# QK-normed attention with a SwiGLU layer behind it: the last four sequences' queries and keys are turned by VectorE and not by TensorE

## The chip, the cores and the metric

The kernel runs on one core of a Trainium2 chip. A core has five engines with a queue of instructions each: TensorE (PE, matmuls into PSUM), VectorE (DVE), ScalarE (ACT), GpSimd (POOL) and SyncE (SP, which here issues DMAs). The queues are in order and wait for each other through semaphores. The metric is the device time of one execution in microseconds; three runs of the kernel before took 1516.35, 1512.67 and 1513.35 us, the median is 1513.35 us. Everything is float32, apart from the weights, which arrive as 64-bit floats.

## The reference, cut to what matters

```python
# attention: 8 sequences, 12 heads, 448 tokens, 64 values to a head
def rmsnorm(x, g):
    rms = np.sqrt(np.mean(x * x, axis=-1, keepdims=True) + 1e-06)
    return x / rms * g
q_n, k_n = rmsnorm(q, g_q), rmsnorm(k, g_k)
scores = matmul(q_n, k_n^T) / sqrt(64)
attn = softmax(scores)                      # over the keys
x = matmul(attn, v)                         # -> 3584 tokens x 768
# SwiGLU layer: 768 -> 1536 -> 768
xn = rmsnorm(x, rms_g)
g = xn @ w_gate
out = (g / (1 + exp(-g)) * (xn @ w_val)) @ w_out
```

For the scores, TensorE contracts over the 64 values of a head. So q and k must lie with these values along the partitions and the tokens along the free axis, while in memory a token's 64 values lie side by side: each head's q and k has to be turned.

## The kernel before, in words

**Steps.** The unit of attention is a pair of heads, g = 0 to 47, six to a sequence (`NPAIR`); two heads of 64 values fill the 128 partitions. The main loop makes one step for each pair. From the second sequence on, step g does, in this order: the scores of pair g (seven parts of 64 keys, `step`, matmuls in L659) interleaved with the value matmuls of pair g-1 (L674); then *items* of the layer behind attention for the sequence before (`fill`), taken from a list that is spread evenly over the steps. Most items are one product of a fast matrix multiplication for gate and value (`product`, L1191: eight PE instructions of 128x224), the others are parts of the output projection (`out_quads`, L1532). Results of items are taken out of PSUM by ScalarE copies (L1206) and VectorE sums (L1209, L1212). Three PSUM banks rotate for items (`ps_f`), four for scores (`ps_s`), and one (`ps_m`) is shared by the value sums and by the turning of q and k.

**How q and k get there, before.** For pair g+3, SP loads q and k with the tokens on partitions (`load_pair`: one DMA for q, two for k; 384 of a head's 448 tokens, three tokens to a partition). The remaining 64 tokens of all heads of a sequence, the *rests*, come in six DMAs once a sequence (L441, L448). For pair g+2, `squares` has ScalarE square q and k (L493), VectorE sum over the 64 values (L496) and GpSimd raise to the power -0.5 (L515) and scale q (`norm_q`, L520); k is scaled by ScalarE in six pieces (`norm_k`, L530). The rests have squares, power and scaling of their own (`norm_rests`). For pair g+1, `turn` transposes on TensorE: three 128x128 blocks of q (L545) and one of the rest (L549), which ScalarE copies out to `qT` with the gains multiplied in (L550) and to `kT` (L551), and later three blocks of k (L545, copied out at L553). The scores become `exp` on ScalarE (L664).

**What sets the order.** The order is written out by hand. `pe(fn)` is one turn of TensorE: it writes fn's instructions into the queues and counts turns. `after(n, fn)` writes fn's instructions into the queues n turns later. No scheduler moves anything afterwards; each engine runs its own queue in the order written. The weights, in the form that the fast multiplication needs, are kept in device memory and stream in through SP (L1070, `w<-kept`, `w<-kept_q`) whenever a buffer comes free. From about 270 us on, each step is such a step.

**DMA semaphores.** DMAs that SP and ScalarE issue take eight semaphores in turn (`DMAHW0` to `DMAHW7`), in the order in which they are written down, whichever queue they are in. A DMA's issue waits until the DMA that had its semaphore before, the eighth before it, has landed.

Of the kernel before, what the change touches and what calls it, by code (L numbers as in the profile page):

```python
# [22 lines left out]
NPAIR = H // 2  # L23
# [312 lines left out]
def safe_scores(  # L336
# [24 lines left out]

    NW = 22
    const, small = pool("c_const", 1), pool("c_small", 4)
    qk_pool, v_pool, qn_pool, qkT_pool = pool("c_qk", 3), pool("c_v", 3), pool("c_qn", 1), pool("c_qkT", 2)
    e_pool, tmp, y_pool, rest_pool = pool("c_e", 11), pool("c_tmp", 1), pool("c_y", 3), pool("c_rest", 2)
# [38 lines left out]

    FULL, LAST = slice(0, NK * 128), slice(NK * 128, S)

    def load_pair(g, parts=(0, 1)):

        if g >= NG:
            return  # L410
        b, hp = divmod(g, NPAIR)
        if 0 in parts:
            qk = st["qk", g] = qk_pool.tile([128, 2, 2 * NK * D], F32, name="qk")
            nc.sync.dma_start(out=qk[:, 0].rearrange("p (h n) -> p h n", h=2),
                              in_=q[b, 2 * hp:2 * hp + 2, FULL].rearrange("h (p t) d -> p h (t d)", t=NK))
        qk = st["qk", g]
        for h in range(2) if 1 in parts else ():
            nc.sync.dma_start(out=qk[:, 1].rearrange("p (t h d) -> p h t d", h=2, d=D)[:, 1 - h],
                              in_=k[b, 2 * hp + h, FULL].rearrange("(p t) d -> p t d", t=NK))

    def load_v(g):
        if g >= NG:
            return
        b, hp = divmod(g, NPAIR)
        vt = st["v", g] = v_pool.tile([128, 2, NK, D], F32, name="vt")
        rows = vt.rearrange("p h t d -> p h (t d)")
        if direct(g):
            nc.sync.dma_start(out=rows, in_=v[b, 2 * hp:2 * hp + 2, FULL].rearrange("h (p t) d -> p h (t d)", t=NK))
            return

        for h in range(2):
            nc.sync.dma_start(out=rows[across(h)], in_=v[b, 2 * hp + h, FULL].rearrange("(f p t) d -> p f (t d)", f=2, t=NK))


    def load_rests(b, i, engine):
        if b >= B:
            return
        if i == 0:
            st["rest", b] = rest_pool.tile([128, NPAIR, 2, D], F32, name="rest")
        for h in range(2):  # L440
            engine.dma_start(out=st["rest", b][own(i), :, 1 - h], in_=(q, k)[i][b, h::2, LAST].rearrange("h i d -> i h d"))  # L441

    def load_v_rests(b):
        if b >= B:
            return
        vr = st["vr", b] = rest_pool.tile([128, NPAIR, D], F32, name="vr")
        for h in range(2):
            nc.sync.dma_start(out=vr[across(h)], in_=v[b, h::2, LAST].rearrange("h i d -> i h d"))  # L448

    def norm_rests(b, lo, hi):  # L450

        if b >= B:
            return
        n = hi - lo
        rest = st["rest", b][:, lo:hi]
        sq = tmp.tile([128, n, 2, D], F32, name="sq", tag="sq", bufs=2)
# [27 lines left out]
    def squares(g, i):  # L484

        if g >= NG:
            return
        n = 2 * NK
        if i == 0:
            st["ms", g] = small.tile([128, 2 * n], F32, name="ms")  # L490
        ms = st["ms", g]
        sq = tmp.tile([128, n * D], F32, name="sq", tag="sq", bufs=2)
        nc.scalar.activation(sq, st["qk", g][:, i], ACT.Square)  # L493

        def reduce():
            nc.vector.tensor_reduce(out=ms[:, i * n:(i + 1) * n], in_=sq.rearrange("p (n d) -> p n d", d=D), axis=AX_X, op=ALU.add)  # L496

        if g <= 1:

            return reduce, lambda: rms_qk(g, slice(i * n, (i + 1) * n))  # L500
        after(1, reduce)
        if i == 1:
            if g == 2:

                due[0:0] = [(now["t"] + 2, lambda: rms_qk(g)), (now["t"] + 2, lambda: norm_q(g))]
                return
            after(2, lambda: rms_qk(g))
            after(2, lambda: norm_q(g))

    def rms_qk(g, cols=slice(0, 4 * NK)):  # L510
        if ("rs", g) not in st:
            st["rs", g] = small.tile([128, 4 * NK], F32, name="rs")
        ms = st["ms", g][:, cols]
        nc.gpsimd.tensor_scalar(ms, ms, D * 1e-6, None, ALU.add)
        nc.gpsimd.tensor_tensor(st["rs", g][:, cols], ms, mhalf[:, cols], ALU.pow)  # L515

    def norm_q(g):
        qn = st["qn", g] = qn_pool.tile([128, 2 * NK * D], F32, name="qn")
        for h in range(2):
            (nc.vector if g <= 2 else nc.gpsimd).tensor_tensor(  # L520
                qn.rearrange("p (t h d) -> p h t d", h=2, d=D)[:, 1 - h], st["qk", g][:, 0].rearrange("p (h t d) -> p h t d", h=2, d=D)[:, h],
                st["rs", g][:, h * NK:(h + 1) * NK].unsqueeze(2).to_broadcast([128, NK, D]), ALU.mult)

    def norm_k(g, half):

        if g >= NG:
            return
        for n in range(NK * half, NK * (half + 1)):
            block = st["qk", g][:, 1, n * D:(n + 1) * D]
            nc.scalar.activation(block, block, ACT.Copy, scale=st["rs", g][:, 2 * NK + n:2 * NK + n + 1])  # L530
# [119 lines left out]
    def keys_of(i):  # L650

        at = i % NK * 128 + i // NK * D if i < 2 * NK else NK * 128
        return slice(at, at + D)

    def scores(g, i):

        ps = ps_s.tile([128, 512], F32, name="sc", tag="s")
        for r in (own(0), own(1)):
            nc.tensor.matmul(ps[r, 0:S], lhsT=st["kT", g][r, keys_of(i)], rhs=st["qT", g][r, :], start=True, stop=True)  # L659
        return ps  # L660

    def exps(g, i, ps):
        e = st["e", g, i] = e_pool.tile([128, S], F32, name="e")
        nc.scalar.activation(e, ps[:, 0:S], ACT.Exp)  # L664

    def weighted(g, i):

# [2 lines left out]
            st["av", g] = ps_m.tile([128, 512], F32, name="av", tag="m")  # L670
        for j in range(2):
            r = across(j)
            vt = st["vr", b][r, hp] if i == PARTS - 1 else st["v", g][r, i // NK, i % NK]
            nc.tensor.matmul(st["av", g][own(j), 0:S], lhsT=vt, rhs=st["e", g, i][r], start=i == 0, stop=i == PARTS - 1,  # L674
                             skip_group_check=True)

# [670 lines left out]
    def store(b, n, i, y):  # L1347
        row0 = at = b * S + i * 128 - 64 * (b % 2)
        while at < row0 + 128:
            seq, col = divmod(at, S)  # L1350
            t, p = divmod(col, 128)
            m = min((128 if t < NK else REST) - p, row0 + 128 - at)
            rows, cols = seq * S, slice(n * HALF, (n + 1) * HALF)
            if t < NK:
# [374 lines left out]
    ones = const.tile([128, D], F32, name="ones")  # L1729
    nc.vector.memset(ones, 1.0)  # L1730

    nc.scalar.activation(tmp.tile([128, D], F32, name="sq", tag="sq", bufs=2), ones, ACT.Square)
    mhalf = const.tile([128, 4 * NK], F32, name="mhalf")
# [32 lines left out]
    def warm(n):  # L1766

        ps = ps_m.tile([128, 512], F32, name="warm", tag="m")
        for _ in range(n):
            nc.tensor.matmul(ps[:, 0:128], lhsT=ident, rhs=ident, start=True, stop=True)  # L1770

    def some_rests(g):
        b, hp = divmod(g, NPAIR)
# [31 lines left out]
    for g in range(NG + 1):  # L1805
# [70 lines left out]
            if g < NG:  # L1876
                later_sums(g, 2)
        st["block"] = now["t"]
        after(2, lambda g=g: load_v(g + 2))
        if hp:  # L1880
            fill()
            norm_k(g + 1, 0)
            squares(g + 2, 0)
            squares(g + 2, 1)
            pe(lambda: turn(g + 1, 0))
            norm_k(g + 1, 1)
            some_rests(g)
            fill()
            pe(lambda: turn(g + 1, 1))
# [5 lines left out]
        pe(lambda: turn(g + 1, 0))  # L1895
# [5 lines left out]
        pe(lambda: turn(g + 1, 1))  # L1901
        fill(len(todo))
        begin(b - 1, 16)
        pe(lambda: norm_x(b - 1))
# [42 lines left out]
```

## Time and profile before

| | |
|---|---|
| median of three runs | 1513.35 us |
| span of the profiled execution | 1514.0 us |
| PE busy | 1478.8 us, 98% |
| VectorE, ScalarE, GpSimd busy | 1037.7, 602.2, 741.3 us |
| DMA engines busy, queue of SP | 69.4% of 16 engines' span |

The page lists each engine's busy time, the chain of work that ended last, and the costliest groups of instructions; queries of the trace give the same for a window, a source line or a tile, and a timeline. A row of a group gives the count, the summed busy time and the mean duration of one instruction. Matmuls overlap in the pipeline, so their durations add up to more than the time they take; start times in the timeline tell what a piece of TensorE work takes. In a timeline, `x8` is a run of eight instructions shown as one row.

### The profile page before, as it was taken

The numbers are of one execution on the slowest core, as the hardware profiler recorded it, in microseconds if no ns is written. First come the engines' busy times: TensorE is split into PE (matmuls) and PEld (weight loads), VectorE is DVE, ScalarE is ACT, GpSimd is POOL, SyncE is SP. The second block draws the span as 40 slices with busy tenths as digits, with TensorE's granted clock in tenths as the row PEclk, the third lists the DMA queues.
The fourth block names the chain that finished last, engine by engine and source line by source line (L and its number), as shares of the span: only waits on it lengthen the run. The fifth ranks groups of instructions, "written<-read, shape, count | busy, mean of one in ns | idle before, by whom it ended". The sixth has DMA issues, their size and how long they took to land.

```text
span 1514.0 us, 25709 instructions
## 1 busy us (share of the span) xinstructions
PE 1478.8 (98%) x8732; PEld 1154.0 (76%) x8732; DVE 1037.7 (69%) x1826; ACT 602.2 (40%) x1377; POOL 741.3 (49%) x708
## 2 busy tenths in 40 slices
PE   8999999999899999999999999999999999999997
PEld 4344445678755888878888888768888789899997
DVE  5788999699944697874568555535668655684664
ACT  6856764344323433234343443443542433101100
POOL 6867997556423454564535643445645731021002
PEclk9999999999999999999999999999999999999999
DMA  7758675776667899996558855585558655587675
GB/s 200 227 159 252 174 247 174 228 249 206 224 219 224 266 316 312 301 291 180 163 150 257 244 176 153 165 255 159 153 153 255 216 162 139 165 292 234 174 228 180
DMA packets 302176, 322.51 MB, mean 213 GB/s; under 512 B 81620, under 2 KB 243668, under 8 KB 302036
## 3 DMA queue, kind: packets, MB, share of 16 engines
q1 hardware_dynamic: 301108, 320.58, 69.4%
q8 instruction: 72, 1.18, 0.3%
q14 instruction: 68, 0.56, 0.1%
q10 hardware_dynamic: 800, 0.20, 0.1%
q0 software_dynamic: 128, 0.00, 0.0%
HBM read 266.90 MB, written 53.77 MB: 212 GB/s over the span
## 4 chain that ended last, share of the span: by engine, by line
PE 84%; DVE 8%; DMA 3%; issue 1%; SPq 1%; POOL 1%; ACT 0%; DVEq 0%; POOLq 0%
PE ff L1191 37%; PE ff L1532 13%; PE sc L659 7%; PE av L674 7%; PE ff L1604 6%; PE ff L1461 5%; PE tr L545 2%; PE den L692 1%; PE den L607 1%; PE sc L563 1%; PE av L590 1%; PE ff L1334 1%; DVE l L1406 1%; DMA w<-kept 1%; DVE w L1091 1%
## 5 line engine op out<-in xcount | busy, mean ns | idle before, releaser
L1191 PE MATMUL ff<-x,w 128*128 128x224 f32 x1296 | 259.6, 353 | 1.4 <-DVE pb L1212 1.1
L714 POOL TENSOR_TENSOR es<-es,e 128x448 f32<-128x448 f32 x205 | 253.4, 1236 | 13.6
L1191 PEld LDWEIGHTS ff<-x,w 128*128 128x128 f32 x1296 | 242.7, 190 | 5.4 <-DVE pb L1212 1.4
L659 PE MATMUL sc<-qT,kT 64*64 64x448 f32 x1176 | 231.0, 539 | 0.7 <-DVE x L744 0.7
L674 PE MATMUL av<-e,vt 64*64 64x448 f32 x984 | 193.1, 538 | 0.0
L664 ACT ACTIVATE e<-sc 128x448 f32<-128x448 f32 x294 | 154.2, 547 | 72.6 <-PE sc L659 57.1
L1191 PE MATMUL ff<-xs,w 128*128 128x224 f32 x832 | 165.0, 353 | 2.9 <-issue 1.6
L1191 PEld LDWEIGHTS ff<-xs,w 128*128 128x128 f32 x832 | 155.7, 190 | 6.2 <-issue 3.0
L644 POOL TENSOR_TENSOR ss<-ss,rd 128x448 f32<-128x448 f32 x40 | 47.1, 1178 | 207.2 <-ACT rd L643 206.5
L709 POOL TENSOR_TENSOR es<-e 128x448 f32<-128x448 f32 x41 | 49.2, 1200 | 192.3 <-ACT e L664 192.3
L659 PEld LDWEIGHTS sc<-qT,kT 64*64 64x64 f32 x1176 | 79.2, 133 | 82.1 <-issue 60.1
L1532 PE MATMUL ff<-w,l 128*128 128x192 f32 x630 | 117.8, 328 | 3.7 <-DVE pa L1567 1.7
L515 POOL TENSOR_TENSOR rs<-ms,mhalf 128x12 f32<-128x12 f32 (+1 forms) x50 | 115.9, 2319 | 4.2
L1212 DVE TENSOR_TENSOR pc<-ff,l 128x448 f32<-128x448 f32 x56 | 34.8, 622 | 115.7 <-PE ff L1191 80.9
L1604 PE MATMUL ff<-x,w 128*128 128x448 f32 x288 | 111.8, 541 | 0.0
L1532 PEld LDWEIGHTS ff<-w,l 128*128 128x128 f32 x630 | 103.8, 190 | 8.7 <-DVE pa L1567 2.9
L674 PEld LDWEIGHTS av<-e,vt 64*64 64x64 f32 x984 | 66.0, 133 | 41.6 <-issue 41.6
L1604 PEld LDWEIGHTS ff<-x,w 128*128 128x128 f32 x288 | 53.3, 190 | 51.1 <-issue 48.2
L1191 PE MATMUL ff<-top_x,w 128*128 128x224 f32 x440 | 91.1, 356 | 0.0
L1209 DVE TENSOR_TENSOR pb<-ff,pb 128x448 f32<-128x448 f32 x84 | 52.3, 623 | 56.1 <-PE ff L1191 50.3
L1191 PEld LDWEIGHTS ff<-top_x,w 128*128 128x128 f32 x440 | 81.8, 190 | 11.3 <-issue 8.5
L1191 PE MATMUL ff<-l,w 128*128 128x224 f32 x416 | 83.6, 353 | 1.1 <-DVE pc L1212 1.1
(212 smaller groups left out, 2806.1 us busy)
## 6 DMA issues: line engine op xcount, KB each, us to landing
w<-kept SPq DMA_DIRECT2D x380, 256.0 KB, 3.5
w<-kept_q SPq DMA_DIRECT2D x350, 192.0 KB, 3.8
w<-kept_o SPq DMA_DIRECT2D x150, 192.0 KB, 3.6
kept_q<-w SPq DMA_DIRECT2D x63, 192.0 KB, 3.9
qk<-in_q_dram SPq DMA_DIRECT2D x48, 192.0 KB, 3.7
qk<-in_k_dram SPq DMA_DIRECT2D x96, 96.0 KB, 3.7
raw<-in_moe_w_gate_dram SPq DMA_DIRECT2D x24, 384.0 KB, 4.8
raw<-in_moe_w_val_dram SPq DMA_DIRECT2D x24, 384.0 KB, 4.4
```

Of the source, the lines that this page charges most:

```text
L515: nc.gpsimd.tensor_tensor(st["rs", g][:, cols], ms, mhalf[:, cols], ALU.pow)
L644: after(m, lambda: (nc.gpsimd.tensor_tensor(ss, ss, rd, ALU.add), st.update({("summed", b): hp})))
L659: nc.tensor.matmul(ps[r, 0:S], lhsT=st["kT", g][r, keys_of(i)], rhs=st["qT", g][r, :], start=True, stop=True)
L664: nc.scalar.activation(e, ps[:, 0:S], ACT.Exp)
L674: nc.tensor.matmul(st["av", g][own(j), 0:S], lhsT=vt, rhs=st["e", g, i][r], start=i == 0, stop=i == PARTS - 1, skip_group_check=True)
L709: nc.gpsimd.tensor_tensor(st["es", g], st["e", g, 0], st["e", g, 1], ALU.add)
L714: nc.gpsimd.tensor_tensor(st["es", g], st["es", g], st["e", g, i], ALU.add)
L1191: nc.tensor.matmul(bank[:, w * HT:(w + 1) * HT], lhsT=data(key)[:, (2 * w + c) * 128:(2 * w + c + 1) * 128], rhs=a[left][:, c, :], start=o ...
L1209: nc.vector.tensor_tensor(T[name], ps[:, 0:S], T[name], ALU.add)
L1461: nc.tensor.matmul(ps, lhsT=left_o(b, which, LEFT_O[name], c), rhs=data(("wo", b, name, c)), start=first and c == 0, stop=c == NFP - 1, sk ...
L1532: nc.tensor.matmul(ps, lhsT=a[:, j, :], rhs=data(key)[:, n % 2 * HW:(n % 2 + 1) * HW], start=start and j == 0, stop=j == KG - 1, skip_grou ...
L1604: nc.tensor.matmul(bank[w][:, 0:S], lhsT=data(key)[:, c * 128:(c + 1) * 128], rhs=st["x", 0][:, 3 * half + c, :], start=half == c == 0, st ...
```

## The change

For the pairs of the last four sequences (g from 24 on, `turned(g)`), q and k take another way:

- **Load.** ScalarE's own DMA queue loads them instead of SP's, in eight DMAs for a pair (`load_turned`): each brings 32 of a head's 64 values for all 448 tokens, as 448 runs of 128 bytes, onto 32 partitions. They are written into ScalarE's queue one a turn, from the fourth turn after the step's begin. There are no rests. v is loaded by SP in four DMAs and not two.
- **Norms.** ScalarE squares q and k (448 columns), VectorE sums over 32 values; the two halves of a head lie on different partitions, so eight small ScalarE copies bring each half's sums beside the other's (`other`), GpSimd adds them, raises to the power -0.5 (21 columns) and scales q in place. k is not scaled at all: its factor goes into `exp` as a scale per partition.
- **Turning.** VectorE transposes 32x32 blocks: q in place, then ScalarE reorders it into `qT` with the gains; k straight into `kT`. TensorE's seven transposes of a pair are gone.
- **Memory.** Five pools become one tile, `yard`, cut up by hand, since the new layout needs other places than the old. The order of the output rows of these sequences is now that of the tokens, which merges some stores.

The core of the diff (left out: `load_v_turned`, the places within `yard`, and renames):

```diff
+    def load_turned(g):
+        b, hp = divmod(g, NPAIR)
+        qk = st["qk", g] = spot(g % 3 * 2 * S, 2 * S).rearrange("p (a n) -> p a n", a=2)
+        def load(i, h, e):
+            to = (1 - h) * D + 32 * e
+            nc.scalar.dma_start(out=blocks(qk[to:to + 32, i]),
+                              in_=(q, k)[i][b, 2 * hp + h].rearrange("(p c) d -> p c d", c=NB)[:, :, 32 * e:32 * e + 32])
+        for n in range(8):
+            after(4 + n, lambda n=n: load(n // 4, n // 2 % 2, n % 2))
...
+    def squares_turned(g):
...
+        for i in range(2):
+            sq = new_sq()
+            nc.scalar.activation(sq, qk[:, i], ACT.Square)
+            after(1, lambda i=i, sq=sq: nc.vector.tensor_reduce(out=ms[:, 0, i * NB:(i + 1) * NB], in_=blocks(sq), axis=AX_X, op=ALU.add))
...
+        def other():
+            for at in (0, 64):
+                nc.scalar.copy(ms[at:at + 32, 1, both], ms[at + 32:at + 64, 0, both])
+                for to, of in ((every, every), (first, second)):
+                    nc.scalar.copy(ms[at + 32:at + 64, 1, to], ms[at:at + 32, 0, of])
+                nc.scalar.copy(ms[at + 32:at + 64, 0, first], ms[at + 32:at + 64, 0, second])
+        def total():
+            nc.gpsimd.tensor_tensor(ms[:, 0, both], ms[:, 0, both], ms[:, 1, both], ALU.add)
+            nc.gpsimd.tensor_scalar(ms[:, 0, both], ms[:, 0, both], D * 1e-6, None, ALU.add)
+        def root():
+            nc.gpsimd.tensor_tensor(rs, ms[:, 0, both], mhalf, ALU.pow)
+            nc.gpsimd.tensor_tensor(blocks(qk[:, 0]), blocks(qk[:, 0]), rs[:, 0:NB].unsqueeze(2).to_broadcast([128, NB, 32]), ALU.mult)
+        after(2, other)
+        after(3, total)
+        after(3, root)
+    def turn_q(g):
...
+        q = st["qk", g][:, 0]
+        nc.vector.transpose(out=blocks(q), in_=blocks(q))
+        after(1, lambda: nc.scalar.activation(st["qT", g].rearrange("p (i n) -> p i n", n=NB), q.rearrange("p (n i) -> p i n", i=32),
+                                              ACT.Copy, scale=gqk[:, 0:1]))
+    def turn_k(g):
...
+        nc.vector.transpose(out=st["kT", g].rearrange("p (n s i) -> p s n i", s=2, i=32),
+                            in_=st["qk", g][:, 1].rearrange("p (s n i) -> p s n i", s=2, i=32))
...
-        nc.scalar.activation(e, ps[:, 0:S], ACT.Exp)
+        if turned(g):
+            nc.scalar.activation(e, ps[:, 0:S], ACT.Exp, scale=st["rs", g][:, NB + i:NB + i + 1])
+        else:
+            nc.scalar.activation(e, ps[:, 0:S], ACT.Exp)
...
+    def turn_for(g, i):
+        if turned(g):
+            (turn_q, turn_k)[i](g)
+        else:
+            pe(lambda: turn(g, i))
```

What moves in the queues is seen in step 33, which is like most of those from step 24 on (`l`, `pa`, `pb`, `pc` are the sums of one group of 15 products; the line numbers behind the change are those of the new file). **TensorE**, the items of that step, before:

```order
L1191 MATMUL ff<-x,w 128x224 x4
L1191 MATMUL ff<-l_7675,w 128x224 x4
L1191 MATMUL ff<-l_7695,w 128x224 x4
L545 MATMUL tr<-ident,qn 128x128 x3
L549 MATMUL tr<-ident,rest 128x128
L1191 MATMUL ff<-x,w 128x224 x20
L545 MATMUL tr<-ident,qk 128x128 x3
L1191 MATMUL ff<-raw,w 128x224 x4
```

and with the change:

```order
L1309 MATMUL ff<-x,w 128x224 x4
L1309 MATMUL ff<-l_7509,w 128x224 x4
L1309 MATMUL ff<-l_7534,w 128x224 x4
L1309 MATMUL ff<-x,w 128x224 x20
L1309 MATMUL ff<-raw,w 128x224 x4
```

The seven transposes are gone and the products close up; nothing else moves on this engine. **ScalarE** in the same items, behind the copy `pb` out of PSUM, before, with the semaphores that each instruction waits for:

```order
L530 ACTIVATE qk<-qk,rs 128x64 [waits Activation_49]
L530 ACTIVATE qk<-qk,rs 128x64 x2
L493 ACTIVATE sq<-qk 128x384 [waits DMAHW4_49]
L493 ACTIVATE sq<-qk 128x384 [waits DMAHW6_49,DMAHW5_49]
L550 ACTIVATE qT<-tr,gqk 128x448 [waits PE_49]
L551 COPY kT<-tr 128x64
L530 ACTIVATE qk<-qk,rs 128x64 x3
L457 ACTIVATE sq<-rest 128x384 [waits DMAHW2_49,DMAHW1_49,DMAHW7_49,DMAHW0_49,DVE_49]
L1219 ACTIVATE th<-pa 128x448 [waits DVE_49]
L1219 ACTIVATE th<-pb 128x448 [waits DVE_49]
L553 COPY kT<-tr 128x384 [waits PE_49]
L1206 COPY l_7745<-ff 128x448 [waits PE_49]
```

and with the change, from that copy on (one DMA stands ahead of it; the other seven small copies, the two `th` and the copy `l` follow):

```order
L1324 COPY pb<-ff 128x448 [waits PE_49]
L440 DMA yard<-in_q_dram 32x14x32 [waits DMAHW0_49]
L440 DMA yard<-in_q_dram 32x14x32 [waits DMAHW3_49]
L440 DMA yard<-in_q_dram 32x14x32 [waits DMAHW5_49]
L440 DMA yard<-in_k_dram 32x14x32 [waits DMAHW0_49]
L440 DMA yard<-in_k_dram 32x14x32 [waits DMAHW3_49]
L463 ACTIVATE sq<-yard 128x448 [waits DMAHW6_49,DMAHW2_49]
L463 ACTIVATE sq<-yard 128x448 [waits DMAHW7_49]
L440 DMA yard<-in_k_dram 32x14x32 [waits DMAHW6_49]
L495 ACTIVATE qT<-yard,gqk 128x448 [waits DVE_49]
L440 DMA yard<-in_k_dram 32x14x32 [waits DMAHW0_49]
L470 COPY yard<-yard 32x21 [waits DVE_49,Pool_49]
```

Six pieces of `norm_k` and two copies of `kT` have gone; eight DMAs, each waiting for one of the eight DMA semaphores, and eight small copies have come, and `qT` waits for VectorE where it waited for TensorE. **VectorE** in the same items, before:

```order
L1212 TENSOR_TENSOR pc<-ff,l_7745 128x448
L496 TENSOR_REDUCE ms<-sq 128x6 x2
L1209 TENSOR_TENSOR pb<-ff,pb 128x448
L1209 TENSOR_TENSOR pa<-ff,pa 128x448 x2
L459 TENSOR_REDUCE msr<-sq 128x6
L1209 TENSOR_TENSOR pb<-ff,pb 128x448
L1209 TENSOR_TENSOR pc<-ff,pc 128x448 x2
```

and with the change:

```order
L1330 TENSOR_TENSOR pc<-ff,l_7586 128x448
L494 STREAM_TRANSPOSE yard<-yard 128x448
L1327 TENSOR_TENSOR pb<-ff,pb 128x448
L464 TENSOR_REDUCE yard<-sq 128x14 x2
L1327 TENSOR_TENSOR pa<-ff,pa 128x448 x2
L1327 TENSOR_TENSOR pb<-ff,pb 128x448
L1327 TENSOR_TENSOR pc<-ff,pc 128x448 x2
L1341 SCALAR_TENSOR_TENSOR h_115<-th,pa 128x448
L1342 SCALAR_TENSOR_TENSOR h_115<-h_115,pa 128x448
L502 STREAM_TRANSPOSE kT<-yard 128x2x7x32
```

Two transposes have come in among the sums that empty PSUM, and the rests' sum of squares is gone.

More of the change, by code (lines that the diff above doesn't have):

```diff
@@ new lines, in load_v_turned @@
+    def load_v_turned(g):
+        b, hp = divmod(g, NPAIR)
+        vt = st["v", g] = spot((AT_QK + 2 * PAIR, AT_V1)[g % 2], S).rearrange("p (n d) -> p n d", d=D)
+        for h in range(2):
+            rows = v[b, 2 * hp + h].rearrange("(p s n) d -> s p n d", s=2, n=NB // 2)
+            for half in range(2):
+                to = across(h).start + 32 * half
+                nc.sync.dma_start(out=vt[to:to + 32], in_=rows[half])
+    def squares_turned(g):
+        qk, n = st["qk", g], 2 * NB
+        ms = st["ms", g] = spot(AT_RS, 2 * n).rearrange("p (a n) -> p a n", a=2)
+        rs = st["rs", g] = spot(AT_RS + (4 + g % 2) * NB + g % 2 * NB // 2, NB + NB // 2)
+        for i in range(2):
+            sq = new_sq()
+            nc.scalar.activation(sq, qk[:, i], ACT.Square)
+            after(1, lambda i=i, sq=sq: nc.vector.tensor_reduce(out=ms[:, 0, i * NB:(i + 1) * NB], in_=blocks(sq), axis=AX_X, op=ALU.add))
+        every, first, second = slice(0, NB), slice(NB, NB + NB // 2), slice(NB + NB // 2, n)
+        both = slice(0, NB + NB // 2)
+        def other():
[13 more added lines that the diff above has]
+        after(3, root)
@@ L1878, in safe_scores @@
         st["block"] = now["t"]
-        after(2, lambda g=g: load_v(g + 2))
+        for n in (1, 2):
+            if turned(g + n) == (n == 1):
+                after(2, lambda g=g + n: load_v(g))
         if hp:
@@ L1882, in safe_scores @@
             norm_k(g + 1, 0)
-            squares(g + 2, 0)
-            squares(g + 2, 1)
-            pe(lambda: turn(g + 1, 0))
+            if not turned(g + 2):
+                squares(g + 2, 0)
+                squares(g + 2, 1)
+            turn_for(g + 1, 0)
+            if turned(g + 2):
+                squares(g + 2, 0)
             norm_k(g + 1, 1)
@@ L1894, in safe_scores @@
         fill(2)
-        pe(lambda: turn(g + 1, 0))
+        turn_for(g + 1, 0)
         norm_k(g + 1, 1)
```

85 lines of the change are left out of this document (63 added, 22 removed).

## The prediction

> **What bounds the kernel now.** I read the page's busy times and chain of waits first, then a table by stretches of the part that the change touches (pairs 24 to 47: their loads begin about 515 us, their last turn is at 1248 us).
>
> ```profile
> PE 1478.8 (98%) x8732; PEld 1154.0 (76%) x8732; DVE 1037.7 (69%) x1826; ACT 602.2 (40%) x1377; POOL 741.3 (49%) x708
> PE 84%; DVE 8%; DMA 3%; issue 1%; SPq 1%; POOL 1%; ACT 0%; DVEq 0%; POOLq 0%
> core 0: us, PE busy (x) PEld busy (x) DVE busy (x) ACT busy (x) POOL busy (x), PEclk, DMA share, GB/s
> 515.00:700.00 185.00, 180.64 (x1180) 154.25 (x1180) 142.75 (x267) 71.06 (x167) 93.77 (x86) 1.00 0.94 298
> 700.00:900.00 200.00, 199.34 (x1317) 170.56 (x1316) 129.38 (x228) 82.84 (x191) 96.25 (x90) 1.00 0.63 192
> 900.00:1100.00 200.00, 199.11 (x1215) 159.28 (x1214) 107.88 (x179) 83.65 (x196) 101.07 (x101) 1.00 0.60 178
> 1100.00:1250.00 150.00, 149.33 (x993) 128.44 (x992) 100.12 (x176) 57.26 (x135) 77.23 (x71) 1.00 0.64 198
> ```
>
> TensorE is the bound: 84% of the chain, and from 515 to 1250 us it is idle for 735 - 728.4 = 6.6 us in all, 4.4 of them before 700 us. There the DMA engines are 94% busy; afterwards 60 to 64%. VectorE has 480.2 us of work in these 735 (65%), ScalarE 294.8 (40%), GpSimd 368.3 (50%). So a microsecond taken off TensorE is a microsecond off the time, if nothing else starts to hold TensorE up.
>
> **TensorE: what is removed.** Each of 24 pairs loses seven transposes. Their price is read from start times in the timeline of TensorE in step 33:
>
> ```profile
> 873.17 0.49 PE L545 MATMUL tr<-ident,qn 128*128 128x128 f32 x3
> 873.50 0.27 PE L549 MATMUL tr<-ident,rest 128*128 128x128 f32 x1
> 873.61 7.73 PE L1191 MATMUL ff<-x,w 128*128 128x224 f32 x40
> 881.18 0.49 PE L545 MATMUL tr<-ident,qk 128*128 128x128 f32 x3
> 881.51 1.68 PE L1191 MATMUL ff<-raw,w 128*128 128x224 f32 x8
> ...
> L545 PE MATMUL tr<-ident,qn x144: 272/273/329, 8.6 to 1247.8; 128*128 128x128 f32 x144
> ```
>
> From the first transpose of q to the next product 0.44 us pass (873.17 to 873.61), for k 0.33 us (881.18 to 881.51). 24 x 0.77 = **18.5 us** less. Forty instructions from 873.61 to 881.18 also give the pace of items: 0.189 us each, a product of eight 1.51 us. The duration of one transpose, 273 ns, would give 168 x 0.273 = 45.9 us; I take the starts, since the next instruction begins 0.11 us after the last. The Trainium skill, TensorE: Matmul & The Clock Gate, Part 4 (PE-mode transpose), puts a 128x128 transpose in a kernel at about 275 ns; the trace has the same duration, but by start times it isn't what TensorE pays, and the sum by that figure would be 1468 us.
>
> **ScalarE.** Rows of its groups (count, busy time, mean), the only DMAs it issues now, and its timeline (`qT` of step 25, step 33, `qT` of step 46):
>
> ```profile
> L664 ACT ACTIVATE e<-sc 128x448 f32<-128x448 f32 x294 | 154.2, 547 | 72.6 <-PE sc L659 57.1 <-PE av L674 6.8 <-PE den L607 2.4
> L530 ACT ACTIVATE qk<-qk,rs 128x64 f32<-128x64 f32 x246 | 67.5, 344 | 0.0
> L567 ACT ACTIVATE e<-sc,rs 128x448 f32<-128x448 f32 x42 | 23.3, 638 | 13.3 <-PE sc L563 13.3
> L553 ACT COPY kT<-tr 128x384 f32<-128x384 f32 x40 | 19.0, 476 | 71.8 <-PE tr L545 71.8
> L551 ACT COPY kT<-tr 128x64 f32<-128x64 f32 x40 | 8.1, 202 | 0.0
> L441 ACTq DMA_DIRECT2D rest<-in_q_dram x2: 639/673/707, 0.7 to 1.5; - x2
> ...
> 631.65 0.61 ACT L550 ACTIVATE qT<-tr,gqk 128x448 f32<-128x448 f32 x1
> ...
> 866.05 0.53 ACT L630 COPY x<-av 128x448 f32<-128x448 f32 x1
> ...
> 873.81 0.63 ACT L550 ACTIVATE qT<-tr,gqk 128x448 f32<-128x448 f32 x1 [4.41 <-PE tr L549]
> ...
> 884.74 0.53 ACT L1206 COPY l<-ff 128x448 f32<-128x448 f32 x1 [2.55 <-PE ff L1191]
> ...
> 1248.26 0.64 ACT L550 ACTIVATE qT<-tr,gqk 128x448 f32<-128x448 f32 x1 [6.29 <-PE tr L549]
> ```
>
> Removed from a step: six pieces of `norm_k` at 67.5/246 = 0.27 us, 1.65; the copies to `kT`, 0.68; a third of a rests' square, 0.18 (as L664). Added: eight DMA issues at 0.67, 5.4 us (I count them in full, as if ScalarE could do nothing beside them); eight small copies between 0.20 (L551) and 0.27 (L530), I take 0.22, 1.8; 64 more columns in each square, at L664's 1.2 ns, 0.2; a scale in seven `exp`, 638 - 547 = 0.09 each, 0.6. The reorder of q takes the place of L550, 0.63; it reads values that lie 128 bytes apart, which no row shows: from 0.63 to twice that, I take the low end, as both read one value a column. Sum +8.0 - 2.5 = 5.5 us a step. A step lasts 29.4 us (from 631.65 to 1248.26 us it is 21 steps), so ScalarE goes from 11.8 to 17.3 us of it. Locally: between the copies at 866.05 and 884.74, 18.7 us, the new queue holds 0.53 + 5.4 + 0.53 (`pb`) + 1.2 (squares) + 0.63 + 1.8 + 1.2 (two `th`) = 11.3 us. One DMA a turn beside one copy is 0.67 + 0.53 = 1.20 us against 1.51 us of TensorE. Cost on the path: nothing, as long as the issues don't wait. ScalarE stood 4.41 us waiting for TensorE's transposes in this step, and that wait goes.
>
> **Waits of the issues.** A DMA is issued when the eighth before it has landed. Landing and load of the queues:
>
> ```profile
> w<-kept SPq DMA_DIRECT2D x380, 256.0 KB, 3.5
> ...
> w<-kept SPq DMA_DIRECT2D x50, 256.0 KB, 4.3
> q1 hardware_dynamic: 37823, 40.71, 91.7%
> ...
> q10 hardware_dynamic: 800, 0.20, 9.8%
> ```
>
> (The first is the whole run, the next two 560 to 700 us, the last ScalarE's two DMAs in the first 9 us.) In step 33 the eighth before lies two to three turns back, 3 to 4.5 us, so with 3.5 us the issue waits 0 to 0.5 us; in the stretch of 4.3 us, up to 1.3 us and more if SP is late. What is queued behind on ScalarE are copies out of PSUM; a product's bank is wanted again after two more products, 3.0 us, less 0.53 for the copy: a wait up to 2.5 us is covered. I put **1 us** in all for waits that pass this, between 0 and 8 (six steps before 700 us, 1.3 us each).
>
> **The DMA engines.** 800 packets in 9.8% of 16 x 9 us are 17.6 ns for a run of 256 bytes. A run of 128 bytes takes between half and all of this; eight DMAs of 448 runs: 3584 x 8.8 to 17.6 / 16 = 2.0 to 3.9 us a pair. Now: 768 runs for k 0.84 us, 256 runs of 768 bytes at most three times that each, 0.84, a sixth of 1536 runs of rests, 0.28: 2.0 us. So 0 to 1.9 us more a pair. After 700 us a third of the engines' time is free and hides it. Before, six pairs are loaded at 94%: 0 to 11.4 us. The stream of weights runs ahead of its use, so I take **4 us**. SP loses three issues a step and a sixth of six, and gains two for v, which helps it.
>
> The Trainium skill, DMA: Bandwidth & Descriptors, Specifications, wants at least 512 bytes a run for the line rate and speaks against 128. No row has 128; at 256 the trace has 17.6 ns, and only where the engines are full can it cost time, which is the first rival.
>
> **VectorE, GpSimd.**
>
> ```profile
> L597 DVE STREAM_TRANSPOSE rd<-rd 128x448 f32<-128x448 f32 x41 | 26.2, 639 | 55.1 <-ACT rd L699 54.8
> L1209 DVE TENSOR_TENSOR pb<-ff,pb 128x448 f32<-128x448 f32 x84 | 52.3, 623 | 56.1 <-PE ff L1191 50.3 <-ACT qk L530 5.6
> L515 POOL TENSOR_TENSOR rs<-ms,mhalf 128x12 f32<-128x12 f32 x46 | 110.5, 2403 | 3.8
> L515 POOL TENSOR_TENSOR rs<-ms,mhalf 128x6 f32<-128x6 f32 x4 | 5.4, 1354 | 0.3
> ```
>
> VectorE gains two transposes, 1.28 us a step, to 20.5 of 29.4; one behind a sum is 0.62 + 0.64 = 1.26 us, less than a product. GpSimd's power goes from 12 columns to 21: 2.4 us and 0.17 a column more, 4.0 us; the rests' share and the smaller pieces about cancel; 50% busy, and its sums are wanted a step later. Both cost nothing; if a transpose is late, the sum behind it is, and the 3.0 us of the banks cover that.
>
> **Sum.** 1514.0 - 18.5 + 4 + 1 = 1500.5 us of span; the median of the runs is 0.65 us under the profiled span, so **1500 us**.
>
> **Rivals.** *The crowded stretch decides* (slower). If a run of 128 bytes costs as much more as the rule fears, twice the 256-byte row, a pair takes 3584 x 35.2 / 16 = 7.9 us of the engines, 5.9 more than now; six pairs that nothing absorbs give 35 us, 1514 - 18.5 + 35 = 1531. It beats the gain from 3.1 us a pair on, 22.8 ns a run. For it: 94% busy, 4.4 us of idle TensorE there already. Against: half the bytes shouldn't take longer. 10%. *ScalarE's queue eats it* (no change): waits of the issues pass the 2.5 us in most steps by about 0.7 us, 24 x 0.7 = 17 us: 1513. For it: eight waits a step that weren't there. Against: 7.4 us to spare in step 33. 12%. *The transposes cost their duration*: 1468 us, with the same 1.51 us a product. The start times are against it: 2%.
>
> **How the numbers follow.** Forecast 76%, 1494 to 1508.8. A measurement here can tell 0.3%, 4.5 us, from no change. Faster: 76 + 2 = 78%; same 12%, slower 10%. Range 1494 (18.5 us and little else, 1495) to 1513 (both unknown costs near their upper ends): it leaves out the slower rival and a tail below.
>
> **What would show it.** After: no L545 rows behind about 570 us; products closing up at 1.51 us; idle TensorE between 515 and 1250 us near 12 us, most before 700. Wrong if TensorE waits for ScalarE copies or `w<-kept` there by more than 18 us, if ScalarE's DMA issues take well over 0.7 us, or if the product's pace changes.

## The result, and the profile after

Median of five runs each, side by side: before 1512.67 us, after **1522.99 us**; the ratio is 1.0055, with a 95% interval of 1.004 to 1.0069. The change makes the kernel slower by about 10 us, where 13 us faster were forecast. The profiled execution has a span of 1521.2 us (before 1514.0), and its own time is the median of the runs.

The busy times, the chain of waits and the table by the same stretches as before:

```profile
PE 1471.2 (97%) x8564; PEld 1142.5 (75%) x8564; DVE 1061.6 (70%) x1866; ACT 615.7 (40%) x1369; POOL 764.1 (50%) x684
PE 76%; DMA 9%; DVE 9%; issue 2%; POOL 1%; ACT 1%; SPq 1%; ACTq 0%; DVEq 0%; POOLq 0%
515.00:700.00 185.00, 167.31 (x1042) 139.05 (x1045) 139.74 (x261) 66.60 (x154) 86.39 (x70) 0.97 0.90 277
700.00:900.00 200.00, 198.14 (x1274) 172.01 (x1267) 136.72 (x238) 83.81 (x187) 111.60 (x92) 1.00 0.74 205
900.00:1100.00 200.00, 196.79 (x1198) 154.48 (x1200) 117.70 (x196) 91.41 (x200) 99.34 (x87) 1.00 0.62 174
1100.00:1250.00 150.00, 148.14 (x986) 125.44 (x977) 105.04 (x187) 64.40 (x142) 86.44 (x71) 1.00 0.69 202
```

TensorE is idle 17.7 us between 515 and 700 us (before 4.4), and its clock there is 0.97 of full speed in place of 1.00. Of the chain it has 8% less, and most of that has gone to DMA. Behind 700 us it is idle 6.9 us (before 2.2).

These rows cut the time by the clock and not by progress. For that, take the start of the first score product of a step, from the trace's records of that line. Step g works on pair g, writes the loads of pair g+3 and turns pair g+1: the first loads of the new kind belong to step 21, and the first pair that VectorE turns to step 23.

```
start of step      21      26      36      47     21 to 26   TensorE idle in it   at half clock in it
before          488.5   647.9   950.4  1263.6      159.4            3.7                 0.0
after           488.1   667.1   963.7  1272.8      178.9           17.0                10.2
```

Two things are read from it. Steps 21 to 25 take 19.5 us longer: 13.3 us of idle TensorE, 10.2 us at half clock (5.1 us of work lost), about 1 us of the rest, though VectorE already turns the first three pairs in them. And from step 26 on the kernel gains 9.9 us in 21 steps, though TensorE is idle 5.2 us more in them: 15.1 us of work are gone, 0.72 a step. The gain is there, and one stretch of five steps, in which three pairs are turned and the loads of the new kind have begun, takes more than all of it. (The first of these loads goes out at 495.5 us; in the kernel before, pair 24 is loaded from 489.8 us on. The 515 us of the prediction are most of a step late.)

What holds TensorE up from 515 to 700 us, longest first, and below the dots the two longest waits of the kernel before in the same window:

```profile
PE msx L844 <- POOL ss L755: 2.8, 1, 2.8
PE ff L1653 <- DVE pc L1673: 2.6, 1, 2.6
PE ff L1653 <- DVE pb L1673: 2.0, 1, 2.0
PE ff L1653 <- DMA w<-kept_q: 1.8, 1, 1.8
PE ff L1653 <- DVE pb L1688: 1.8, 1, 1.8
PE ff L1309 <- DMA w<-kept: 1.7, 3, 0.8
...
PE ff L1191 <- DMA w<-kept: 1.3, 1, 1.3
PE ff L1532 <- DMA w<-kept_q: 1.3, 1, 1.3
```

Of the 17.7 us, 10.6 name VectorE, whose sums in these rows take 0.35 us (L1673) and 0.55 us (L1688) each, as before. The timelines of ScalarE and TensorE at the same place show who was late (ACTq rows are DMA issues and the waits among them):

```profile
637.84 7.05 ACTq L440 DMA_DIRECT2D yard<-in_q_dram  x4
645.01 0.32 ACT L1672 COPY th<-ff 128x192 f32<-128x192 f32 x1 [10.45 <-DMA yard<-in_q_dram]
...
645.77 1.24 PE L1653 MATMUL ff<-w,raw 128*128 128x192 f32 x6 [1.97 <-DVE pb L1673]
```

Four DMA issues spread over 7.05 us stand ahead of the copy `th<-ff`. It starts 10.45 us after ScalarE's last work, VectorE's sum `pb` waits for it, and TensorE waits 1.97 us for `pb`. In the kernel before, such a copy of the same step waits for TensorE:

```profile
637.16 0.32 ACT L1551 COPY th<-ff 128x192 f32<-128x192 f32 x1 [4.07 <-PE ff L1532]
```

The chain of waits, 10 us later, goes back over two DMAs of SP:

```profile
646.21 3.72 DMA w<-kept_q
...
649.99 4.61 DMA w<-kept_q
...
654.62 0.57 ACTq L440
...
656.81 0.33 ACT th L1672
657.14 0.03 issue
657.16 0.37 DVE pc L1673
657.53 0.04 issue
657.57 0.43 PE ff L1653
```

A load of weights lands, SP issues another, that one lands at 654.60, and 0.02 us later ScalarE's issue goes out; behind it come the small copies, `th`, the sum, and TensorE after 2.65 us of idling. ScalarE's DMA didn't need those weights. It needed the semaphore that the load of weights held. Each of the 194 DMAs of ScalarE and 1529 of SP takes one of eight semaphores in the order in which the program was written, and the program gives each issue a wait on the one it takes. Set against the landings in the trace:

```
ScalarE's issue      wait before it   the DMA with that semaphore before      issue after its landing
563.74 q                  2.56        SP  kept_q<-w   558.78, landed 563.72        0.02
570.40 q                  1.87        SP  w<-kept     564.83, landed 570.38        0.02
600.52 q                  4.97        SP  w<-kept     596.09, landed 600.50        0.02
643.59 q                  2.80        SP  w<-kept_q   638.78, landed 643.57        0.02
654.62 k                  0.35        SP  w<-kept_q   649.99, landed 654.60        0.02
all of 500 to 680 us     37.1         33.1 of it end at such a landing
```

Of the 33.1 us, 8.4 end at the landing of one of ScalarE's own loads, the others at one of SP's.

### The profile page after: what moved, and what is told of

Its sections match the earlier page's. It is cut to its first block, busy times and chain, and to the rows that moved or that the text cites. A ratio compares the mean times of both kernels' runs of the same rounds, so it can differ in the third digit from the quotient of the medians.

```text
span 1521.2 us, 25575 instructions
## 1 busy us (share of the span) xinstructions
PE 1471.2 (97%) x8564; PEld 1142.5 (75%) x8564; DVE 1061.6 (70%) x1866; ACT 615.7 (40%) x1369; POOL 764.1 (50%) x684
## 3 DMA queue, kind: packets, MB, share of 16 engines
q10 hardware_dynamic: 89888, 11.22, 4.8%
## 4 chain that ended last, share of the span: by engine, by line
PE 76%; DMA 9%; DVE 9%; issue 2%; POOL 1%; ACT 1%; SPq 1%; ACTq 0%; DVEq 0%; POOLq 0%
PE ff L1309 33%; PE ff L1653 11%; PE sc L774 7%; PE av L792 7%; PE ff L1725 6%; PE ff L1582 5%; DMA w<-kept_o 2%; DMA w<-kept_q 2%; DMA w<-kept 1%; DMA kept_q<-w 1%; DMA yard<-in_q_dram 1%; PE den L810 1%; PE den L718 1%; PE sc L674 1%; PE av L701 1%
## 5 line engine op out<-in xcount | busy, mean ns | idle before, releaser
L1309 PEld LDWEIGHTS ff<-x,w 128*128 128x128 f32 x1296 | 245.9, 192 | 8.6 <-DVE pb L1327 2.2
L792 PE MATMUL av<-e,yard 64*64 64x448 f32 x1148 | 223.9, 538 | 0.0
L755 POOL TENSOR_TENSOR ss<-ss,rd 128x448 f32<-128x448 f32 x40 | 47.5, 1186 | 178.1 <-ACT rd L754 177.4
L792 PEld LDWEIGHTS av<-e,yard 64*64 64x64 f32 x1148 | 77.5, 133 | 50.0 <-issue 50.0
L1653 PEld LDWEIGHTS ff<-w,l 128*128 128x128 f32 x630 | 104.7, 191 | 13.3 <-DVE pb L1688 3.8
L780 ACT ACTIVATE e<-sc,yard 128x448 f32<-128x448 f32 x168 | 102.2, 636 | 29.7 <-PE sc L774 21.5
L480 POOL TENSOR_TENSOR yard<-yard,mhalf 128x21 f32<-128x21 f32 x24 | 91.0, 3791 | 2.0
L1725 PEld LDWEIGHTS ff<-x,w 128*128 128x128 f32 x288 | 53.3, 190 | 51.1 <-issue 48.2
L1624 POOL TENSOR_TENSOR y<-y,pa 128x384 f32<-128x384 f32 x10 | 11.4, 1157 | 152.8 <-DVE y L1700 152.8
```

The source lines that it names most:

```text
L480: nc.gpsimd.tensor_tensor(rs, ms[:, 0, both], mhalf, ALU.pow)
L755: after(m, lambda: (nc.gpsimd.tensor_tensor(ss, ss, rd, ALU.add), st.update({("summed", b): hp})))
L780: nc.scalar.activation(e, ps[:, 0:S], ACT.Exp, scale=st["rs", g][:, NB + i:NB + i + 1])
L1309: nc.tensor.matmul(bank[:, w * HT:(w + 1) * HT], lhsT=data(key)[:, (2 * w + c) * 128:(2 * w + c + 1) * 128], rhs=a[left][:, c, :], start=o ...
L1653: nc.tensor.matmul(ps, lhsT=a[:, j, :], rhs=data(key)[:, n % 2 * HW:(n % 2 + 1) * HW], start=start and j == 0, stop=j == KG - 1, skip_grou ...
L1725: nc.tensor.matmul(bank[w][:, 0:S], lhsT=data(key)[:, c * 128:(c + 1) * 128], rhs=st["x", 0][:, 3 * half + c, :], start=half == c == 0, st ...
```

## Experiments

Three theories for the stretch: **queue** (the issues of the loads stand in line, and what stands behind them is late), **traffic** (runs of 128 bytes fill the DMA engines), **work** (VectorE and GpSimd have too much to do there). Ratios are to the kernel before, run beside.

### Where the loss is: five kept, and six pairs without loads

```diff
-    TURNED = 4
+    TURNED = 5
```

> The switch to turned loads comes one sequence later: five sequences keep the old way and three are turned, so that the first turned load is issued in step 27 (about 700 us) and not in step 21 (515 us). Three theories for the 21 us that steps 19 to 23 lose in the changed kernel. QUEUE: ScalarE's DMA issues wait for semaphores that they share with SP's late weight loads, and ScalarE's copies behind them come late. TRAFFIC: the 128-byte runs fill the DMA engines, and weights land late. WORK: VectorE's and GpSimd's added work makes them late where VectorE has most to do. All three place the loss in the crowded stretch from 515 to 700 us, and expect 18 pairs at 0.77 us as gain and almost no loss: 1513 - 14 = 1499 us (1497 to 1503). The rival SWITCH, that the first turned pairs cost 21 us wherever they lie (the hand-over of the buffers), expects 1513 - 14 + 21 = 1520 us.

1503.81 us, ratio 0.9926 (0.9904 to 0.9948): 10.8 us faster than before, the first clear gain. The loss belongs to the place, not to the switch. (By the pair that they work on, the steps that lose are 21 to 25; the expectation calls them 19 to 23.) The row of the stretch is that of before again (181.13 us of TensorE work, DMA 0.94):

```profile
515.00:700.00 185.00, 181.13 (x1183) 154.87 (x1183) 141.85 (x267) 71.13 (x166) 92.68 (x85) 1.00 0.94 296
```

Three of the 13.9 us are missing, most of them in small waits for VectorE behind 700 us.

```diff
-        for n in range(8):
+        for n in range(8 if g >= (TURNED + 1) * NPAIR else 0):
             after(4 + n, lambda n=n: load(n // 4, n // 2 % 2, n % 2))
```

> The changed kernel without the 48 q and k loads of its first six turned pairs, which are issued in steps 21 to 26 (the arithmetic runs on what stands in the buffers; those pairs are not the reference's). QUEUE and TRAFFIC: the loss of the crowded stretch goes, 1502 to 1506 us; they cannot be told apart by this run. WORK: 1518 to 1523 us.

1505.24 us, 0.9942 (0.9924 to 0.9959). Steps 21 to 25 take 159.6 us, as before (159.4), with TensorE idle 4.2 us. All the arithmetic of the change is still there, the turning of three pairs in these steps too, so **work** alone does not make the loss in the stretch; it takes the 48 loads, which cost 17 us by the ratios, 18 by the medians.

### What about the loads: their queue, their runs, their number

```diff
-            nc.scalar.dma_start(out=blocks(qk[to:to + 32, i]),
+            nc.sync.dma_start(out=blocks(qk[to:to + 32, i]),
```

> The changed kernel with its eight q and k loads a step issued by SP in place of ScalarE; bytes, runs and arithmetic stay. QUEUE: ScalarE waits for no semaphore of a DMA any more; of the 21 us most comes back, less what SP loses by eight issues of 0.6 us a step: 1503 to 1510 us. TRAFFIC: the packets are the same, 1521 to 1526 us. WORK: 1521 to 1526 us.

1516.41 us, 1.0013 (1.0002 to 1.0024): 6.6 us come back, half of the least that **queue** expected. ScalarE issues none of these loads now, and they stand in SP's line instead, ahead of the weights. In the profiled execution (1511.86 us) the longest waits of TensorE between 515 and 700 us are:

```profile
PE ff L1309 <- DMA w<-kept: 4.4, 2, 3.3
PE ff L1309 <- DVE pb L1327: 2.2, 1, 2.2
```

```diff
-            nc.scalar.dma_start(out=blocks(qk[to:to + 32, i]),
-                              in_=...rearrange("(p c) d -> p c d", c=NB)[:, :, 32 * e:32 * e + 32])
+            nc.scalar.dma_start(out=qk[to:to + 32, i],
+                              in_=...rearrange("(p c) d -> p (c d)", c=NB)[:, S * e:S * e + S])
```

> The changed kernel with each of the 192 turned loads reading the same number of bytes into the same 32 partitions in runs of 1792 bytes in place of fourteen of 128 bytes (the values then stand in the wrong places, so the attention of the last four sequences is not the reference's). Issues, queue, semaphores and arithmetic stay. QUEUE: the issues still wait, 1519 to 1524 us. TRAFFIC: the loss goes, 1502 to 1508 us. WORK: 1521 to 1524 us.

1514.58 us, 0.9998 (0.9982 to 1.0014), between the two. In the profiled execution (1517.32 us) steps 21 to 25 have TensorE idle 16.3 us (17.0 with short runs), and ScalarE waits 39.5 us before its issues between 500 and 680 us (37.1). What differs is that no half clock falls into the stretch (5.1 of the 6.0 us by which it is shorter), that 1.2 us and not 8.4 of ScalarE's waiting end at landings of its own loads, and that an issue takes 0.32 us and not 0.57:

```profile
L440 ACTq DMA_DIRECT2D yard<-in_q_dram x96: 317/346/1549, 495.9 to 1188.2; - x96
...
L440 ACTq DMA_DIRECT2D yard<-in_q_dram x96: 567/582/999, 495.5 to 1194.5; - x96
```

(The first row is of this kernel, the second of the changed one.) How the 8 us split between these three isn't settled, and a part for **traffic** is not excluded.

```diff
-        for n in range(8):
-            after(4 + n, lambda n=n: load(n // 4, n // 2 % 2, n % 2))
+        for n in range(2):      # one load for all of q of the pair, one for k, 1792-byte runs
+            after(4 + 4 * n, lambda n=n: load(n))
```

> The changed kernel with two loads a step on ScalarE's queue in place of eight: all of q of a pair in one, all of k in the other, in 1792-byte runs (values in the wrong places; the bytes are the same). QUEUE: in the traces so far 33 of the 37 us that ScalarE stands before these issues between 500 and 680 us end 0.02 us after the landing of the DMA that had the same semaphore before, so a quarter of the issues should bring most of the 18 us back: 1503 to 1509 us. TRAFFIC: what long runs alone brought stays, about 1514 us.

1509.48 us, 0.9971 (0.9959 to 0.9983), 0.5 us over what **queue** expected and, with the same bytes, 4 us (by the ratios) to 5 us (by the medians) under long runs alone: fewer issues cost less. (Each load is also four times as wide, on 128 partitions and not 32, which this run doesn't separate.) ScalarE still waits 23.4 us at its ten issues between 500 and 680 us.

The disputed cost by itself, in the kernel **before**:

```diff
+    small_loads = const.tile([32, 64], F32, name="small_loads")
...
+        for n in range(8 if g >= 4 * NPAIR else 0):
+            after(4 + n, lambda n=n: nc.scalar.dma_start(out=small_loads[0:32, 8 * n:8 * n + 8], in_=q[b, 2 * hp, 0:32, 0:8]))
```

> The kernel before, with eight small loads a step added on ScalarE's queue (32 partitions of 32 bytes, into a tile that nothing reads), from step 21 on at the places of the turned loads; TensorE turns as before. QUEUE: the issues alone cost the crowded stretch 8 to 20 us and the steps behind it nothing: 1521 to 1533 us. TRAFFIC: 8 KB a step are nothing, 1513 to 1516 us. WORK: 1513 to 1516 us.

1526.80 us, 1.0083 (1.0051 to 1.0115). Eight loads of 1 KB a step, which nothing reads, cost 12 us. By progress it is steps 21 to 25 again: 168.8 us for 159.4; from step 27 to 36 the distance to before stays at 9.1 to 9.2 us. Before the forty small issues of the stretch ScalarE waits 35.3 us (39.9 before those of the changed kernel), and 25.2 of them end at the landing of a load of SP (26.4). So the price is that of the issues and their waits, with next to no traffic, and nearly all of it is paid in the stretch.

```diff
-            nc.scalar.dma_start(out=blocks(qk[to:to + 32, i]),
+            nc.gpsimd.dma_start(out=blocks(qk[to:to + 32, i]),
```

> The changed kernel with its eight q and k loads a step issued by GpSimd, whose loads take no semaphore of the eight that SP and ScalarE share. QUEUE: no shared wait is left, 1502 to 1509 us, as long as GpSimd's own issues do not make its sums late (no row so far prices one; GpSimd is busy 94 of 185 us between 515 and 700 us). TRAFFIC: the packets are the same, 1520 to 1526 us.

1518.53 us, 1.0025 (1.0012 to 1.0037): a miss for **queue** as it stood. No shared semaphore is left, and TensorE is still idle 12.2 us in steps 21 to 25. GpSimd now works 0.63 us for each load, and VectorE is busy longer with the same operations, 116.0 us in steps 22 to 25 (111.2 in the run without the 48 loads):

```profile
515.00:700.00 185.00, 170.38 (x1102) 142.29 (x1101) 150.72 (x265) 70.74 (x162) 115.48 (x117) 1.00 0.91 286
```

Nor were the packets the same, as the text expected: that queue moved 2.52 MB in 1402 of them between 515 and 700 us, 1.8 KB each. So the theory has to be wider than the shared semaphores. In steps 22 to 25 of the kernel before, VectorE is busy 106.8 of 128.0 us (83%, against 65% over the whole part) and SP's issues fill 95.6; ScalarE, busy 47.5 us, has room, but what stands behind a waiting issue can't use it. On ScalarE's line the loads hold up VectorE's operands, on SP's line the weights. On GpSimd's they lengthen GpSimd's own work and VectorE's; which of the two TensorE waits for there no run separates.

### Where in the order they stand

```diff
-            after(4 + n, lambda n=n: load(n // 4, n // 2 % 2, n % 2))
+            after(4, lambda n=n: load(n // 4, n // 2 % 2, n % 2))
```

> The changed kernel with the eight loads of a step issued one behind the other at one place of ScalarE's order (where the first stood) in place of eight places. QUEUE: each issue still takes the semaphore of the eighth DMA before it, but the eight of them find the last eight of SP's, so that ScalarE stands once a step for about one landing (4 to 5 us) in place of about 8 us in pieces: 1513 to 1519 us, between two loads and eight. If the pieces do not matter but where ScalarE's copies stand behind them, either side of that.

1655.63 us, 1.0918 (1.0895 to 1.094): 133 us slower than the changed kernel, where 4 to 10 faster were expected. ScalarE waits before its issues for about the same time as there (40.9 us in steps 21 to 25, against 39.9), but in one block, which the eight issues themselves lengthen by 0.6 us each. A quiet step, timeline of ScalarE and then of TensorE:

```profile
842.59 2.59 ACTq L440 DMA_DIRECT2D yard<-in_q_dram  x4
846.73 5.86 ACTq L440 DMA_DIRECT2D yard<-in_k_dram  x4
852.69 1.04 ACT L754 ACTIVATE rd<-x 128x448 f32<-128x448 f32 x2 [9.49 <-DMA yard<-in_k_dram]
...
857.91 1.65 PE L844 MATMUL msx<-ones,ss 128*112 128x1 f32 x8 [6.19 <-POOL ss L755]
```

ScalarE starts no operation for ten microseconds (9.49 of them idle), and TensorE stands 6.2. In the changed kernel the quiet steps have as much waiting (71.0 us before the issues from 700 to 1210 us) and lose next to nothing by it, where a copy can slip in between two issues. On top, the clock is 0.958 over the span.

```diff
-            after(4 + n, lambda n=n: load(n // 4, n // 2 % 2, n % 2))
+            after(3 + 3 * n, lambda n=n: load(n // 4, n // 2 % 2, n % 2))
```

> The changed kernel with the eight loads of a step three places apart in ScalarE's order in place of one. In one block they cost 133 us and in eight neighbouring pieces 10, with about the same 35 us of standing between 500 and 680 us, so what counts is how long ScalarE stands at a stretch before a copy that TensorE is about to need. QUEUE, in this form: smaller pieces, of which the slack between ScalarE's copies takes up more: 1508 to 1516 us. If the sum of the standing decided: 1519 to 1525 us.

1519.72 us, 1.0029 (1.0011 to 1.0046): outside what smaller pieces should give, inside the other range. ScalarE's waiting didn't shrink (44.9 us in 500 to 680); in steps 21 to 25, 31.8 of its 41.4 us ended at landings of SP's loads. These steps take 171.4 us, 7.5 less than with neighbouring places, but the 21 steps behind them 612.5 and not 605.7: what the spread gains in the stretch it loses again behind it. (A step has some ten places, so the later loads of a pair come behind the squares that read them; these then take the values that stood there before.) With five kept:

> Five sequences kept and the loads three places apart. Behind 700 us the standing already costs nothing, so the spread should bring nothing more: 1502 to 1505 us, as with neighbouring places (1503.8).

1507.39 us, 0.9948 (0.9931 to 0.9965), 2.4 us over the range; the interval overlaps that of neighbouring places. Over the whole kernel nothing speaks for the spread.

### The kernel that beats both

> Five sequences kept, three turned, and their loads issued by SP in place of ScalarE. QUEUE: behind 700 us the queues have room, and whose queue issues decides nothing: 1502 to 1506 us, as with ScalarE. A rival, that the queue of ScalarE costs something everywhere, expects 1498 to 1501 us.

1503.69 us, 0.993 (0.9913 to 0.9946), as with ScalarE (1503.81): behind the stretch the queue decides nothing.

> Six sequences kept, two turned: 12 pairs at 0.77 us are 9.2 us of TensorE time. Five kept measured 10.8 us below before where 18 pairs are worth 13.9, so 3 us are lost in small waits for VectorE. If these come with each pair (0.17 us a pair): 1513 - 7 = 1506 to 1508 us. If they belong to the first pairs alone or to one place: 1504 to 1506 us, hardly slower than five kept.

(TURNED = 6.) 1509.76 us, 0.9971 (0.9959 to 0.9983), over both ranges: 4.4 us of 9.2. Of four, five and six kept, five is the best, by either queue. By the medians neither account of the small waits fits: the 18 pairs lost 3.1 us, these 12 lost 4.8, and why they keep less than half isn't settled.

## Why the prediction was wrong, step by step

- **TensorE, -18.5 us: right.** 0.77 us a step was forecast, 0.72 measured over 21 steps, with the items at the same pace (forty instructions, five products, take 7.57 us from 917.79 to 925.36 us, 0.189 each). The rival of full durations, 1.91 us a step, falls.
- **Waits of the issues, 1 us between 0 and 8: the step that failed.** The mechanism stood there (an issue waits for the landing of the eighth DMA before it) and was sized with SP on time: up to 1.3 us an issue. Measured: up to 5.0, and 37.1 us between 500 and 680 us. In steps 21 to 25 TensorE stood idle 13.3 us longer and lost 5.1 us of work by the clock, for which the sum had no term; without the 48 loads the loss was gone, and in the kernel before, eight small loads a step cost 12 us alone. The sentence "and more if SP is late" named the case and didn't price it. The three engines wait in a ring there: ScalarE's issues for SP's loads, VectorE for ScalarE's copies, and SP's line for VectorE (first row, 515 to 700 us; the second is SP held by a load of ScalarE; the last is the first row's fellow in the kernel before).

```profile
SPq L1282 <- DVE w L1275: 11.5, 7, 3.6
...
SPq L1282 <- DMA yard<-in_q_dram: 6.4, 2, 3.3
...
SPq L1164 <- DVE w L1157: 5.5, 6, 3.5
```

- **The cover of 2.5 us: wrong in the stretch.** It assumed that VectorE, behind ScalarE, has room. Over 515 to 1250 us it is 65% busy, but in steps 22 to 25 of the kernel before it is 83%, 106.8 of 128.0 us, and the timeline at 645 us shows a delay of it that reached TensorE.
- **DMA engines, 4 us: price right, share of the loss open.** A run of 128 bytes takes 13.0 ns (89888 packets, 4.8% of 16 x 1521.2 us), so a pair 2.9 us, in the middle of the range. From 515 to 700 us the median landing of `w<-kept` is 4.6 us before and after; longer runs left TensorE's idle time there as it was (16.3 us for 17.0), yet made the kernel 8 us faster. The rule on 512 bytes of the Trainium skill (DMA: Bandwidth & Descriptors, Specifications) can't be what decided the most here: eight loads of 1 KB a step in the kernel before cost 12 us.
- **ScalarE's busy time: near, and beside the point.** Issue 0.57 to 0.58 us (0.67 forecast), small copies 0.20 (0.22), `exp` with a scale 0.64; the reorder takes 1.08 us, near the high end of 0.63 to 1.26, not the low one. It had the room. What it lacks is a way to pass a waiting issue.
- **VectorE and GpSimd at nothing: 5 us short.** Transposes 0.63 and the power 3.8 us as forecast, but TensorE idles 5.2 us more in steps 26 to 46, 3.5 of it for VectorE in pieces of up to 0.6 us, the rest for ScalarE.
- **The rivals.** "The crowded stretch decides" had the place right, and its cause, the bytes, is at most a part; "ScalarE's queue eats it" had the cause right and the place wrong: from 700 to 1210 us 71 us of waiting cost next to nothing. Each was costed alone; the case was the two together. Of the signs named ahead, idle TensorE between 515 and 1250 us was to be near 12 us; it is 735 - 710.4 = 24.6, put down mostly to VectorE, with ScalarE behind it. None of the three signs of being wrong appeared: TensorE's waits put down to ScalarE or to `w<-kept` are 4.8 us of the 18 named, an issue takes 0.57 us, and the pace of a product stayed. The loss came by VectorE and by the clock, which none of them watched.

## What to carry to other kernels

A DMA that an engine issues stands in that engine's line like an instruction: look for what it must wait for (here a semaphore shared with another engine's DMAs) and for who needs the instruction behind it, above all where that other engine runs late. Size such waits in the stretch where they fall, by the engines' busy time by progress, not over the whole part that the change touches; here beginning the same change 188 us later turned 10 us of loss into 11 us of gain. If a stall is unavoidable, cut it into pieces between the instructions that others wait for: in steps 21 to 25 the same 40 us of waiting cost 13 us of idle TensorE in pieces, 43 in one block a step. Spreading the pieces further brought nothing more here, and issuing the loads from another engine brought back only part of the loss: 6.6 us from SP, 4.5 from GpSimd.

## What the runs showed of the hardware

**A pause of 2 us costs more than itself.** Half clock comes in windows of 3.413 us on one grid that runs through the whole execution. Windows of the changed kernel:

```profile
603.79:607.20 3.41, 0.57 (x5) 0.28 (x3) 3.41 (x4) 0.00 (x0) 3.33 (x4) 1.00 0.93 221
607.20:610.61 3.41, 3.41 (x14) 3.19 (x14) 3.38 (x6) 0.52 (x1) 3.17 (x4) 0.50 0.45 113
610.61:614.03 3.42, 3.42 (x11) 3.09 (x10) 3.01 (x8) 2.14 (x7) 2.08 (x2) 0.50 0.76 203
614.03:617.44 3.41, 3.41 (x21) 3.36 (x20) 2.49 (x6) 1.80 (x7) 2.34 (x3) 1.00 0.66 200
...
648.16:651.57 3.41, 1.78 (x11) 1.49 (x10) 3.41 (x5) 1.04 (x2) 2.91 (x3) 1.00 1.01 294
651.57:654.99 3.42, 3.19 (x18) 2.90 (x18) 1.58 (x4) 1.07 (x1) 0.00 (x0) 1.00 1.06 323
654.99:658.40 3.41, 0.83 (x5) 0.83 (x6) 1.24 (x4) 1.72 (x9) 1.36 (x3) 1.00 0.97 243
658.40:661.81 3.41, 3.41 (x13) 3.41 (x12) 3.30 (x8) 0.00 (x0) 3.33 (x2) 0.50 0.83 258
```

2.84 us idle in one window, and the next two run at half clock; 1.6 us idle (648.16) and nothing follows; 2.6 us, and half clock again. Over the 14 traces of this case (their last 10 us left out) all 44 full-speed windows with 2.0 us or more of idle TensorE were followed by one at half clock, and of the others only two (1.48 and 1.86 us). The Trainium skill, TensorE: Matmul & The Clock Gate, Part 1, tells of this free-running window of 3413 ns, and the grid agrees; it asks for an idle window, where here 2.0 us of 3.41 were enough. So each pause over that mark costs 1.7 us more for every window that TensorE then fills: in the changed kernel 5.1 us, about half of what it lost against before. The pause of 1.97 us at 643.81 us lies across a border of the grid (644.75), and nothing follows it. That the clock follows the pauses, and not the other way, is read from the order in time; no run changed the clock alone.

**ScalarE reads values 128 bytes apart more slowly.** The reorder of q takes 1.08 us for 448 columns; the copy that it replaces, of the same size from the transposes' bank, took 0.61 to 0.64. That it is the stride and not the memory is read from the square of the same tile, as large and read in order, at 0.57 (second row):

```profile
L495 ACT ACTIVATE qT<-yard,gqk x24: 1071/1084/1113, 575.6 to 1259.0; 128x448 f32<-128x448 f32 x24
...
L463 ACT ACTIVATE sq<-yard 128x448 f32<-128x448 f32 x48 | 25.0, 568 | 73.9 <-DMA yard<-in_q_dram 43.3 <-DMA w<-kept_q 11.9 <-DMA w<-kept 6.2
```
